# Second part's weights decoded during the attention pairs and kept in DRAM; last output products of the first part in two banks

## The chip, the cores and the metric

One core of a Trainium2 chip runs the whole program. The metric is device time in microseconds (us); the kernel before has a median of 967.74 us over 3 runs. Matmuls run on TensorE (PE), elementwise work on VectorE (DVE), ScalarE (ACT) and GpSimd (POOL); SyncE (SP) issues nearly all DMAs.

## The reference, cut to what matters

```python
# 1. attention: B=4, H=8, S=768, D=48, a recurrence over t
cur = einsum('bhd,bhe->bhde', u * k_t, v_t)
y_t = einsum('bhd,bhde->bhe', r_t, state + cur)
state = w_t[..., None] * state + einsum('bhd,bhe->bhde', k_t, v_t)
# 2. first part, x = y as [3072, 384], d_ff 1536
x = (sigmoid(x @ w_gate) * (x @ w_val)) @ w_out
# 3. second part, d_ff 2048
h = x @ w_in;  g = h * tanh(softplus(h));  out = g @ w_out2
```

The weights arrive as 64-bit floats. The kernel has no 64-bit arithmetic: it rebuilds each weight from the two 32-bit words and stores it as two fp16 numbers (a high part and the rest), with three products where one would do.

## The kernel before, in words

**Stages.** The sequence is cut into 24 steps of 32 tokens, two steps make a pair, and 12 pairs (p = 0 to 11) run one behind another. While the gates of pair p are computed, the attention of pair p + 1 is. For each pair there are 12 gates (`gate(p, f)`, 18 matmuls each, L880, then sigmoid L891 and cast L908 on ACT, product L896 and rest L911 on DVE). The output products of the pair before (`out1(p - 1, c, part)`, L944) run between the gates: three column blocks c of four parts each, accumulated in one PSUM bank, `po`. Each block is split into two fp16 halves (`xo`, L212 on ACT, L215 on DVE) and stored in the DRAM tensor `x2d`; the next block can only start when `xo` has left the bank.

**Attention of a pair.** Products and sums of the short-range part on POOL and DVE (L486, L506), transposes on DVE, scaled copies (L623), scores `lp` on PE (L638), copies of them into `X` on ACT and DVE in turn (L655), rows out `yp` on PE (L728), split `xs` (L212, L215), a transposing DMA on ACT's queue into `xt` (L762), and the state `s`: outer products `kp` on PE (L824), added on DVE (L835), decayed on POOL or DVE (L804).

**Second part.** `open_a` gives the space of the attention's short-range tiles to `wi` (tile `wis`), `open_b`, behind all of the attention, gives the rest to `wp` (tile `wps`), the x tiles and two more PSUM pools. `tail_end()`, called in pair 10, loads and decodes `wi` (8 blocks) and then `wp` (8 blocks, each also combined into the seven operands of a Strassen-like product). `h_unit(r, f)` (L1054) and `out2(r, m, h)` (L1169) then use them.

**Decoding a block** (`load_raw`, `decode`, `combine`): a 768 KB DMA (L267); two ACT passes, `word` (L248) and `low` (L238); a DVE join (L292); for `wi` a cast (L303, ACT or DVE) and a difference (L306, POOL or DVE); for `wp` three sums (L332, `sum_wp`, on POOL or DVE), three casts (L346) and three differences (L332, `wps`).

**Order.** `Plan` is a list scheduler written out in the kernel. Each step is added with an engine (or a choice of engines with costs), a cost, a latency `lat` that follows it, and the keys it reads and writes. `run()` works out how late each step may start, counted back from the end, then gives each engine's next free time to the ready step that is due first, and finally emits all steps by planned begin. On the chip each engine then takes its instructions strictly in that order. `SEM = 0.1` us is the usual latency between steps.

Of the kernel before, what the change touches and what calls it, by code (L numbers as in the profile page):

```python
# [19 lines left out]
NP = NJ // 2  # L20
# [17 lines left out]
SG = 64.0  # L38
SG2 = 64.0
NPT = 32  # L40
NRAW = 1
YPOS = (4, 7)
SEM = 0.1
SHARED = (0,)
WHOLE = range(1, 12, 2)
COLD = 1.9
PARTS = ((), (0,), (1,), (2, 3))
# [2 lines left out]
ENGS = ("pool", "dve")  # L50
W1HI = {"act": 0.83}
W1LO = {"dve": 1.6, "pool": 1.85}
W2HI = {"act": 0.83, "dve": 0.7}
W2LO = {"pool": 1.65, "dve": 0.92}
HD = DM // 2
ORDER = ("11", "12", "S2", "S3", "S1", "22", "S4")
OPERAND = {"11": 0, "12": 1, "S4": 2, "S1": 3, "S3": 4, "S2": 5, "22": 6}
# [102 lines left out]
def mixer_moe_kernel(  # L160
# [30 lines left out]
    pp = sa.enter_context(tc.tile_pool(name="pp", bufs=1, space=PS, side="right"))  # L191

    x2d = dram.tile([NP, KC, 128, 2, NT], F16, name="x2d")
    floor3 = keep.tile([128, 1], F32, name="floor3")
    wgs = w1p.tile([128, 2, KC, F1], F16, name="wgs")
    wvs = w1p.tile([128, 2, KC, F1], F16, name="wvs")
# [62 lines left out]
        npg[0] += 1  # L259
        return ("pg", npg[0] % n)  # L260

    def load_raw(key, pool, src, n, slot, reads=()):
# [6 lines left out]
        add("sp", 2.2, go, reads, [("raw", slot)], lat=2.0)  # L269

    def decode(key, dst, n, count, slot, reads, high_on, lo_on, halves=False, blocks=None):
# [28 lines left out]

        def high(e):
            put = nc.scalar.copy if e == "act" else nc.vector.tensor_copy
            put(out=dst()[:, 0], in_=words[key])  # L303

        def rest(e):
            engines[e].tensor_tensor(  # L306
                out=dst()[:, 1], in0=words.pop(key), in1=dst()[:, 0], op=ALU.subtract
            )

        full = 1.15 if key[0] == "wo" else 0.95  # L310
        add("act", 0.78, rebase, [raw, "consts", "table1"], [word])
        add("act", 1.1, bits3, [raw, "consts"], [low])
        add("dve", full, join, [low], [word])
        if halves:
            combine(key, dst, word, low, reads, high_on, lo_on, count)
            return
        made = [[(key[0], f, a) for f in blocks or [key[1]]] for a in range(2)]
        add(high_on, 0, high, [word, *reads], made[0])
        add(lo_on, 0, rest, [word, *made[0]], made[1])

    def combine(key, dst, word, low, reads, high_on, lo_on, count):
# [12 lines left out]
        def differ(e):  # L334
            sums[key] = t = dp.tile(
                [128, 4, HD], F32, tag=f"low{count % 2}", name=f"sum_{key[0]}{key[1]}"
            )
            w = words[key]
            sub(e, t[:, :2], w[:, :, HD:], w[:, 0].rearrange("p (t d) -> p t d", t=2))
            sub(e, t[:, 2], w[:, 1, HD:], t[:, 0])  # L340
            sub(e, t[:, 3], w[:, 1, :HD], t[:, 2])

        def high(e, n):
            copy = nc.scalar.copy if e == "act" else nc.vector.tensor_copy
            out = dst()[:, 0, 0] if n == 0 else dst()[:, 0, put(n)]
            copy(out=out, in_=blocks(n))  # L346

        def rest(e, n):
            ab = [dst()[:, a, 0] if n == 0 else dst()[:, a, put(n)] for a in range(2)]
            sub(e, ab[1], blocks(n), ab[0])  # L350

        add({"pool": 1.8, "dve": 1.1}, 0, differ, [word], [low])
        for n, part in ((0, 0.25), (1, 0.5), (2, 1.0)):
            src = low if n == 2 else word
            cost = {e: c * part + 0.1 for e, c in high_on.items()}
            add(cost, 0, lambda e, n=n: high(e, n), [src, *reads], [(*key, 0, n)])
            cost = {e: c * part + 0.1 for e, c in lo_on.items()}
            add(cost, 0, lambda e, n=n: rest(e, n), [src, (*key, 0, n)], [(*key, 1, n)])

    def decode_early(name, i, dst, src, count):  # L360

# [504 lines left out]
    def gate(p, f):  # L866
# [63 lines left out]
        add("dve", 0.35, rest, [ps, (*G, 0)], [(*G, 1)])  # L930

    def out1(p, c, part):
        last = p == NP - 1
        bank = "po2" if last and c == 1 else "po"
        cs = slice(128 * c, 128 * c + 128)
        fr = range(3 * part, 3 * part + 3)

# [56 lines left out]
    def open_a(e):  # L994

        sf.close()
        w2["i"] = sb.enter_context(tc.tile_pool(name="w2i", bufs=1))
        w2["wi"] = w2["i"].tile([128, 2, KC, F2], F16, name="wis")

    def open_b(e):  # L1000
        sa.close()
        w2["p"] = sb.enter_context(tc.tile_pool(name="w2p", bufs=1, side="right"))
        w2["raw"] = sb.enter_context(tc.tile_pool(name="raw", bufs=1, side="right"))
        w2["ph"] = sb.enter_context(tc.tile_pool(name="ph", bufs=1, space=PS, side="right"))
        w2["po"] = sb.enter_context(tc.tile_pool(name="po2", bufs=1, space=PS, side="right"))
        w2["wp"] = w2["p"].tile([128, 2, 7, NF2 // 2, HD], F16, name="wps")
        w2["h"] = sb.enter_context(tc.tile_pool(name="hp", bufs=1, side="right"))

    homes = []
    spare = list(range(78))  # L1010
# [30 lines left out]
    def h_unit(r, f):  # L1041
# [1 line left out]
        k = nh[0] % 4  # L1043
        nh[0] += 1
        E = ("e", k)
        fs = slice(128 * f, 128 * f + 128)

        def sums(e):
            t = pg.tile([128, 2, NT], F32, tag=f"pg{ps[1]}", name=f"h{r}_{f}")
# [2 lines left out]
            for a, c in ((0, 0), (0, 1), (1, 0)):  # L1052
                for kc in range(KC):
                    nc.tensor.matmul(  # L1054
                        hps[r, f],
                        w2["wi"][:, a, kc, fs],
                        x2[r][:, c, kc, :],
                        start=(n == 0),
                        stop=(n == 3 * KC - 1),
                    )  # L1060
                    n += 1
# [5 lines left out]
        w = [("wi", f // 2, a) for a in range(2)]  # L1067
        add("pe", 1.95, sums, [*w, ("x2", r % 2)], [ps])
        add("act", 0.62, unit, [ps, "table2", "open"], [E])

# [73 lines left out]
    def out2(r, m, h):  # L1144
# [13 lines left out]
        def sums(e):  # L1158
# [8 lines left out]
            for i in range(NF2 // 2):  # L1167
                for a, c in ((0, 0), (1, 0), (0, 1)):
                    nc.tensor.matmul(  # L1169
                        ops2[h, first],  # L1170
                        home(slots[r, i, name])[:, c, tsl],
                        w2["wp"][:, a, w, i, :],
                        start=(new and n == 0),
                        stop=(n == 3 * NF2 // 2 - 1),
                        skip_group_check=not new,
# [19 lines left out]

        if m == 0 and h == 0:
            add("none", 0, start, [], [O])
        n = {0: 0, 1: 1, 2: 1}.get(w, 2)
        reads = [("slot", slots[r, i, name], c) for i in range(NF2 // 2) for c in range(2)]
        reads += [("wp", i, a, n) for i in range(NF2 // 2) for a in range(2)]  # L1200
# [83 lines left out]
    def tail_end():  # L1284
# [1 line left out]
        done += [("pt", i) for i in range(5)] + [("A", i) for i in range(8)] + ["A"]  # L1286
        add("none", 0, open_a, [], [*done, "opened"])
        for i in range(8):
            cs = slice(256 * i, 256 * i + 256)
            dst = lambda cs=cs: w2["wi"][:, :, :, cs]  # L1290
            load_raw(("wi", i), lambda: dp, in_cols(wi, cs), (KC, 256), i % 3)
            decode(("wi", i), dst, (KC, 256), i, i % 3, ["opened"], W2HI, W2LO)
        add("none", 0, open_b, [], ["attention", "open"])
        for i in range(8):
            cs = slice(2 * i, 2 * i + 2)
            dst = lambda i=i: w2["wp"][:, :, :, i]
            slot = (i + 2) % (3 + NRAW)
            pool = (lambda: dp) if slot < 3 else (lambda: w2["raw"])
            reads = [] if slot < 3 else ["open"]
            load_raw(("wp", i), pool, in_rows(wo2, cs), (2, DM), slot, reads)  # L1300
            decode(("wp", i), dst, (2, DM), i, slot, ["open"], W2HI, W2LO, True)

    cells = {0: fine(0)}
    tail1(0)
# [2 lines left out]
    for p in range(NP):  # L1307
        for f in range(NF1):
# [94 lines left out]
```

## Time and profile before

| | us |
|---|---|
| median of 3 runs | 967.74 |
| lowest, highest | 966.28, 967.86 |
| the profiled execution, its own time | 966.43 |
| its span, first to last instruction | 964.7 |

The page says how long each engine was busy; the list of windows says it stretch by stretch, with the granted clock of TensorE; the list of waits says what PE's idle time ended with. A matmul's duration contains the time it spends in the pipeline, so 18 matmuls of 256 columns issue in about 2 us though each is listed with some 0.27 us.

### The profile page before, as it was taken

How to read it: one execution, taken by the hardware profiler on the slowest of the kernel's cores; microseconds unless marked ns; L12 is line 12 of the kernel's file. 1: busy time of each engine (PE TensorE's matmuls, PEld its weight loads, DVE VectorE, ACT ScalarE, POOL GpSimd, SP SyncE). 2: the span in 40 equal slices, each digit the busy share in tenths (PEclk: the TensorE clock that was granted, in tenths of full speed). 3: DMA queues.
4: the chain of work that ended last, by engine and by line, in shares of the span. 5: the costliest groups of instructions: out<-in, count | busy, mean ns of one | idle time of the engine just before them, and what ended most of it. 6: DMA issues, size and time to landing. Idle time of an engine off the chain costs nothing.

```text
span 964.7 us, 29601 instructions
## 1 busy us (share of the span) xinstructions
PE 895.7 (93%) x12808; PEld 715.9 (74%) x12808; DVE 663.6 (69%) x1202; ACT 496.4 (51%) x1191; POOL 490.7 (51%) x534
## 2 busy tenths in 40 slices
PE   0667899999999999999999889999999999999998
PEld 0455678888888888888888777657767676776788
DVE  7889976767676757686778798875565655556541
ACT  2757864343525344343536566775565655656540
POOL 7999832626464545546364365654343443444330
PEclk9988899999999999999999999999999999999999
DMA  9445832322232323133223760010100102000000
GB/s 307 152 139 163 265 115 75 65 67 72 68 57 72 83 62 76 50 75 71 60 41 101 169 204 12 8 43 1 38 30 10 58 1 66 2 9 26 1 34 34
DMA packets 56467, 71.92 MB, mean 75 GB/s; under 512 B 20752, under 2 KB 37648, under 8 KB 56208
## 3 DMA queue, kind: packets, MB, share of 16 engines
q1 hardware_dynamic: 39696, 66.09, 23.6%
q10 hardware_dynamic: 16640, 3.94, 2.1%
q8 instruction: 100, 1.64, 0.7%
q14 instruction: 31, 0.25, 0.1%
HBM read 56.64 MB, written 9.44 MB: 68 GB/s over the span
## 4 chain that ended last, share of the span: by engine, by line
PE 72%; DVE 13%; ACT 7%; POOL 3%; issue 2%; ACTq 2%; DMA 1%; SPq 0%; DVEq 0%; POOLq 0%
PE gv L880 20%; PE h L1054 19%; PE o L1169 17%; PE o L944 10%; PE yp L728 3%; ACT X L655 2%; ACTq L762 2%; ACT KK L697 2%; DVE X L655 1%; DVE A L506 1%; PE lp L638 1%; POOL pt L486 1%; DVE gt L911 1%; PE kp L824 1%; DVE s L835 1%
## 5 line engine op out<-in xcount | busy, mean ns | idle before, releaser
L1054 PE MATMUL h<-x,wis 128*128 128x512 f16 x864 | 199.9, 379 | 0.0
L486 POOL TENSOR_TENSOR blk<-blk 128x384 f32<-128x384 f32 (+2 forms) x139 | 129.4, 943 | 97.6 <-DMA blk<-rkw 69.9
L880 PE MATMUL gv<-xt,wgs 128*128 128x256 f16 x1296 | 165.9, 278 | 12.3 <-DVE gt L911 11.9
L944 PE MATMUL o<-gt,wos 128*128 128x256 f16 x1296 | 165.2, 273 | 5.9 <-DVE xo L215 5.9
L1088 POOL TENSOR_TENSOR sum<-e 128x256 f32<-128x256 f32 x96 | 71.5, 744 | 186.3 <-ACT e L1065 186.2
L880 PE MATMUL gv<-xt,wvs 128*128 128x256 f16 x1296 | 163.6, 276 | 2.5 <-DVE wvs L306 1.2
L880 PEld LDWEIGHTS <-wgs 128*128 128x128 f16 x1296 | 126.3, 100 | 31.4 <-issue 12.9
L1054 PEld LDWEIGHTS <-wis 128*128 128x128 f16 x864 | 83.5, 98 | 82.9
L944 PEld LDWEIGHTS <-wos 128*128 128x128 f16 x1296 | 126.0, 98 | 24.5 <-issue 6.8
L880 PEld LDWEIGHTS <-wvs 128*128 128x128 f16 x1296 | 125.0, 99 | 20.9 <-DVE wvs L306 1.5
L486 POOL TENSOR_TENSOR pt<-blk 128x384 f32<-128x384 f32 x93 | 105.4, 1157 | 47.0 <-DMA blk<-rkw 43.6
L891 ACT ACTIVATE sig<-gv 128x256 f32<-128x256 f32 x144 | 53.5, 385 | 118.2 <-PE gv L880 114.3
L1065 ACT ACTIVATE e<-h 128x512 f32<-128x512 f32 x96 | 57.2, 596 | 84.6 <-PE h L1054 83.7
L911 DVE TENSOR_TENSOR gt<-gv,gt 128x256 f16<-128x256 f32 x144 | 58.8, 417 | 51.6 <-ACT gt L908 50.1
L908 ACT CAST gt<-gv 128x256 f16<-128x256 f32 x144 | 52.6, 371 | 75.9 <-DVE gv L896 55.3
L896 DVE SCALAR_TENSOR_TENSOR gv<-gv,sig 128x256 f32<-128x256 f32 x144 | 60.7, 431 | 29.3 <-ACT sig L891 28.8
L1169 PE MATMUL o<-wps,gt 128*128 128x192 f16 x612 | 74.0, 246 | 0.0
L655 ACT COPY X<-lp 24x64 f32<-24x64 f32 x174 | 44.5, 256 | 38.2 <-DVE X L655 28.1
L1107 DVE SCALAR_TENSOR_TENSOR gt<-e,gt 128x256 f16<-128x256 f32 x41 | 27.3, 675 | 49.6 <-ACT gt L1102 49.6
L506 DVE TENSOR_REDUCE A<-pt 128x32 f32<-128x768 f32 (+1 forms) x60 | 51.4, 863 | 12.3 <-POOL pt L486 12.3
L1169 PE MATMUL o<-wps,wgs 128*128 128x192 f16 x498 | 59.4, 246 | 0.0
L1169 PE MATMUL o<-wps,wos 128*128 128x192 f16 x456 | 57.1, 246 | 0.0
(106 smaller groups left out, 1508.4 us busy)
## 6 DMA issues: line engine op xcount, KB each, us to landing
v<-vt SPq DMA_DIRECT2D x96, 96.0 KB, 3.3
blk<-rkw SPq DMA_DIRECT2D x22, 384.0 KB, 3.5
raw_wi<-wi SPq DMA_DIRECT2D x8, 768.0 KB, 4.8
raw_wp<-wo SPq DMA_DIRECT2D x8, 768.0 KB, 6.2
blk<-rkw SPq DMA_DIRECT2D x11, 512.0 KB, 4.0
raw_wg<-wg SPq DMA_DIRECT2D x6, 768.0 KB, 6.2
raw_wv<-wv SPq DMA_DIRECT2D x6, 768.0 KB, 6.1
raw_wo<-wo SPq DMA_DIRECT2D x6, 768.0 KB, 4.7
```

The source lines that it names most:

```text
L486: engines[e].tensor_tensor(out=pv, in0=a, in1=b, op=ALU.mult)
L506: nc.vector.tensor_reduce(out=cell(), in_=shape(pts.pop(n)), op=ALU.add, axis=AX.X)
L655: put(out=xp[p][rs, xs, t:], in_=lps[p, e][rs, :, c : c + C - t])
L880: nc.tensor.matmul(gps[p, f][:, o], w[:, a, kc, fs], xt[p][:, c, kc, :], start=(n == 0), stop=(n == 3 * KC - 1),)
L891: nc.scalar.activation(out=sgs[p, f], in_=gps[p, f][:, 0], func=AF.Sigmoid, scale=1.0 / (SW * SX))
L896: nc.vector.scalar_tensor_tensor(out=gps[p, f][:, 1], in0=gps[p, f][:, 1], scalar=SG / (SW * SX), in1=sgs.pop((p, f)), op0=ALU.mult, op1=A ...
L911: nc.vector.tensor_tensor(out=gt[p][:, 1, f], in0=gps[p, f][:, 1], in1=gt[p][:, 0, f], op=ALU.subtract,)
L944: nc.tensor.matmul(ops[p, c][:, :NT], wos[:, a, f, cs], gt[p][:, g, f, :], start=(f == 0 and n == 0), stop=(f == NF1 - 1 and n == 2),)
L1054: nc.tensor.matmul(hps[r, f], w2["wi"][:, a, kc, fs], x2[r][:, c, kc, :], start=(n == 0), stop=(n == 3 * KC - 1),)
L1065: nc.scalar.activation(out=es[r, f], in_=hps[r, f], func=AF.Mish, scale=ih)
L1088: engines[e].tensor_tensor(out=sums[0][:, n - 1], in0=a(), in1=b(), op=op)
L1169: nc.tensor.matmul(ops2[h, first], home(slots[r, i, name])[:, c, tsl], w2["wp"][:, a, w, i, :], start=(new and n == 0), stop=(n == 3 * NF2 ...
```

## The change

The decode steps of `wi` and `wp` move from `tail_end()` into pairs 3 to 9, counted from 0 (the 4th to the 10th). One block is started every five gates, behind the gate's rest (`("tick", p, f)`). It is decoded into a staging tile (tag `raw2`), stored in a DRAM scratch (`wid`, `wpd`) and fetched from there when the space of the second part is open. The decode steps get `lat = SLACK = 3.0` in the plan, so that the steps that follow each other are planned at least 3 us apart. The casts are fixed to ACT, the differences and sums to POOL. The fourth raw slot goes. The tiles `wis` and `wps` get their block number as the first free dimension. Of the output products of pairs 10 and 11 every other block uses bank `po2`.

```diff
-NRAW = 1
+AHEAD = 3
+SLACK = 3.0
-W2HI = {"act": 0.83, "dve": 0.7}
-W2LO = {"pool": 1.65, "dve": 0.92}
+W2HI = {"act": 0.83}
+W2LO = {"pool": 1.65}
+    wid = dram.tile([8, 128, 2, KC, 256], F16, name="wid")
+    wpd = dram.tile([8, 128, 2, 7, HD], F16, name="wpd")
...
-        add("act", 0.78, rebase, [raw, "consts", "table1"], [word])
-        add("act", 1.1, bits3, [raw, "consts"], [low])
-        add("dve", full, join, [low], [word])
+        add("act", 0.78, rebase, [raw, "consts", "table1"], [word], lat)
+        add("act", 1.1, bits3, [raw, "consts"], [low], lat)
+        add("dve", full, join, [low], [word], lat)
...
-        add({"pool": 1.8, "dve": 1.1}, 0, differ, [word], [low])
+        add("pool", 2.4, differ, [word], [low], lat)
...
+    def decode_ahead(name, i, src, n, made, store, tick):
+        key = (name, i)
+        count = 8 * (name == "wp") + i
+        slot = count % 2
+        stage = ("raw", 2)
...
+        add("none", 0, new, [], [stage])
+        load_raw(key, lambda: dp, src, n, slot, [tick], 3 * SLACK)
+        decode(
+            key, lambda: tiles[0], n, count, slot, [stage], W2HI, W2LO, name == "wp", None, SLACK
+        )
...
+        add(
+            "sp",
+            0.6,
+            lambda e: nc.sync.dma_start(out=store[i], in_=tiles[0]),
+            [*parts, stage],
+            [(name, "stored", i)],
+            lat=2.0,
+        )
...
     def out1(p, c, part):
-        last = p == NP - 1
-        bank = "po2" if last and c == 1 else "po"
+        bank = "po2" if p > NP - 3 and (KC * p + c) % 2 else "po"
...
+    def fetch(name, src, i, opened):
+        def go(e):
+            nc.sync.dma_start(out=w2[name][:, i], in_=src[i])
+
+        made = [(name, i)]
+        add("sp", 0.6, go, [(name, "stored", i), opened], made, lat=2.5)
...
         for i in range(8):
-            cs = slice(256 * i, 256 * i + 256)
-            dst = lambda cs=cs: w2["wi"][:, :, :, cs]
-            load_raw(("wi", i), lambda: dp, in_cols(wi, cs), (KC, 256), i % 3)
-            decode(("wi", i), dst, (KC, 256), i, i % 3, ["opened"], W2HI, W2LO)
+            fetch("wi", wid, i, "opened")
         add("none", 0, open_b, [], ["attention", "open"])
         for i in range(8):
...
-            load_raw(("wp", i), pool, in_rows(wo2, cs), (2, DM), slot, reads)
-            decode(("wp", i), dst, (2, DM), i, slot, ["open"], W2HI, W2LO, True)
+            fetch("wp", wpd, i, "open")
...
+            n, rem = divmod(NF1 * (p - AHEAD) + f, 5)
+            if rem == 2 and 0 <= n < 16:
+                ahead(n, ("tick", p, f))
```

## Rows read from the trace of the kernel before

**Rows 1.** The page, part 1: busy time of the engines, share of the span.
```profile
PE 895.7 (93%) x12808; PEld 715.9 (74%) x12808; DVE 663.6 (69%) x1202; ACT 496.4 (51%) x1191; POOL 490.7 (51%) x534
```

**Rows 2.** Windows: length; busy PE, PEld, DVE, ACT, POOL; clock; DMA share; GB/s.
```profile
160.00:344.00 184.00, 183.12 (x3426) 158.73 (x3423) 130.89 (x245) 76.13 (x215) 93.94 (x98) 1.00 0.27 68
344.00:505.00 161.00, 158.57 (x3195) 136.61 (x3195) 113.28 (x218) 65.53 (x188) 86.26 (x90) 1.00 0.27 63
505.00:560.00 55.00, 51.50 (x849) 44.26 (x847) 43.84 (x74) 33.35 (x72) 20.43 (x18) 1.00 0.58 148
560.00:597.00 37.00, 32.74 (x297) 28.80 (x295) 33.43 (x53) 22.18 (x45) 26.02 (x27) 1.00 0.28 92
597.00:964.70 367.70, 364.45 (x2988) 261.18 (x2986) 208.62 (x405) 199.38 (x465) 147.03 (x192) 1.00 0.08 24
```

**Rows 3.** What PE waited for from 344 to 505 us: total, times, longest.
```profile
PE yp L728 <- DVE s L835: 1.3, 4, 0.6
PE yp L728 <- DVE RD L623: 1.0, 2, 0.6
```

**Rows 4.** The same from 505 to 560 us, then from 560 to 597 us.
```profile
PE gv L880 <- issue: 1.6, 2, 1.2
PE yp L728 <- issue: 1.4, 2, 0.7
PE yp L728 <- DVE s L835: 0.5, 2, 0.3
...
PE o L944 <- DVE xo L215: 4.3, 3, 2.3
```

**Rows 5.** Groups by shape from 160 to 505 us: one per gate.
```profile
L911 DVE TENSOR_TENSOR gt<-gv,gt 128x256 f16<-128x256 f32 x94 | 38.1, 417 | 42.5 <-ACT gt L908 41.0
```

**Rows 6.** Timeline of ACT and PE in pair 2 (153 to 158 us).
```profile
154.94 1.01 ACT L238 ACTIVATE low_wi<-raw_wi,floor 128x768 uint32<-128x768 uint16 x1
...
157.94 0.27 PE L944 MATMUL o<-gt,wos 128*128 128x256 f16 x1 [0.95 <-DVE xo L215]
```

**Rows 7.** Groups by shape, whole span: decode steps, count, busy, mean ns, idle before.
```profile
L306 POOL TENSOR_TENSOR wis<-word_wi,wis 128x768 f16<-128x768 f32 x6 | 10.1, 1684 | 19.8 <-DVE wis L303 14.7 <-ACT wis L303 5.1
L332 POOL TENSOR_TENSOR sum_wp<-word_wp,sum_wp 128x192 f32<-128x192 f32 x16 | 11.9, 745 | 1.3
L332 POOL TENSOR_TENSOR sum_wp<-word_wp 128x384 f32<-128x384 f32 x8 | 8.9, 1116 | 13.1 <-DVE word_wp L292 13.1
L332 POOL TENSOR_TENSOR wps<-sum_wp,wps 128x768 f16<-128x768 f32 x3 | 5.5, 1818 | 0.9 <-ACT wps L346 0.9
L238 ACT ACTIVATE low_wi<-raw_wi,floor 128x768 uint32<-128x768 uint16 x8 | 8.1, 1011 | 4.8 <-issue 4.7
```

**Rows 8.** Tile word_wi: count, duration ns min/median/max, first and last start.
```profile
L292 DVE SCALAR_TENSOR_TENSOR word_wi<-word_wi,low_wi x8: 947/1127/2404, 150.2 to 540.9; 128x768 uint32<-128x768 uint32 x8
L303 ACT CAST wis<-word_wi x2: 832/836/840, 520.6 to 543.3; 128x768 f16<-128x768 f32 x2
```

**Rows 9.** Groups by shape from 505 to 560 us: a decode step, the gate's cast.
```profile
L248 ACT ACTIVATE word_wi<-raw_wi 128x768 f32<-128x768 f32 x6 | 5.5, 916 | 0.0
L908 ACT CAST gt<-gv 128x256 f16<-128x256 f32 x13 | 4.6, 374 | 5.3 <-DVE word_wi L292 3.0 <-DVE gv L896 2.2
```

**Rows 10.** Timeline of one attention, without decode steps (347 to 351 us).
```profile
347.86 1.67 ACT L655 COPY X<-lp 24x64 f32<-24x64 f32 x6 [0.24 <-PE lp L638]
349.80 0.15 PEld L728 LDWEIGHTS yp<-v,X 64*32 64x32 f32 x8 [0.21 <-ACT X L655]
```

**Rows 11.** Tile xt: landing min/median/max from 160 to 560 us, then from 505 us.
```profile
DMA to landing us min/median/max: 2.3/4.0/8.9
...
DMA to landing us min/median/max: 5.1/7.0/8.9
```

**Rows 12.** Timeline of ACT and PE in pair 7: the last sends, the next pair's first gate.
```profile
409.62 2.59 ACTq L762 DMA_TRANSPOSE xt<-xs  x2
...
421.05 2.13 PE L880 MATMUL gv<-xt,wgs 128*128 128x256 f16 x18
```

More of the change, by code (lines that the diff above doesn't have):

```diff
@@ L260, in next_pg, with load_raw @@
         return ("pg", npg[0] % n)
-    def load_raw(key, pool, src, n, slot, reads=()):
+    def load_raw(key, pool, src, n, slot, reads=(), lat=2.0):
         def go(e):
@@ L267, in go, with decode @@
             nc.sync.dma_start(out=raws[key], in_=src)
-        add("sp", 2.2, go, reads, [("raw", slot)], lat=2.0)
-    def decode(key, dst, n, count, slot, reads, high_on, lo_on, halves=False, blocks=None):
+        add("sp", 2.2, go, reads, [("raw", slot)], lat=lat)
+    def decode(key, dst, n, count, slot, reads, high_on, lo_on, halves=False, blocks=None, lat=SEM):
         raw = ("raw", slot)
@@ L310, in decode, with combine @@
         full = 1.15 if key[0] == "wo" else 0.95
-        add("act", 0.78, rebase, [raw, "consts", "table1"], [word])
-        add("act", 1.1, bits3, [raw, "consts"], [low])
-        add("dve", full, join, [low], [word])
+        add("act", 0.78, rebase, [raw, "consts", "table1"], [word], lat)
+        add("act", 1.1, bits3, [raw, "consts"], [low], lat)
+        add("dve", full, join, [low], [word], lat)
         if halves:
-            combine(key, dst, word, low, reads, high_on, lo_on, count)
+            combine(key, dst, word, low, reads, high_on, lo_on, count, lat)
             return
         made = [[(key[0], f, a) for f in blocks or [key[1]]] for a in range(2)]
-        add(high_on, 0, high, [word, *reads], made[0])
-        add(lo_on, 0, rest, [word, *made[0]], made[1])
-    def combine(key, dst, word, low, reads, high_on, lo_on, count):
+        add(high_on, 0, high, [word, *reads], made[0], lat)
+        add(lo_on, 0, rest, [word, *made[0], *reads], made[1], lat)
+    def combine(key, dst, word, low, reads, high_on, lo_on, count, lat):
         sums = {}
@@ L355, in combine, with new @@
             cost = {e: c * part + 0.1 for e, c in high_on.items()}
-            add(cost, 0, lambda e, n=n: high(e, n), [src, *reads], [(*key, 0, n)])
+            add(cost, 0, lambda e, n=n: high(e, n), [src, *reads], [(*key, 0, n)], lat)
             cost = {e: c * part + 0.1 for e, c in lo_on.items()}
-            add(cost, 0, lambda e, n=n: rest(e, n), [src, (*key, 0, n)], [(*key, 1, n)])
+            add(cost, 0, lambda e, n=n: rest(e, n), [src, (*key, 0, n), *reads], [(*key, 1, n)], lat)
+    def decode_ahead(name, i, src, n, made, store, tick):
[3 more added lines that the diff above has]
+        stage = ("raw", 2)
+        tiles = []
+        def new(e):
+            t = dp.tile([128, 3072], F16, tag="raw2", name=f"made_{name}{i}")
+            size = 2
+            for k in made:
+                size *= k
+            names = "abcd"[: len(made) + 1]
+            dims = {x: k for x, k in zip(names, (2, *made))}
+            tiles.append(
+                t[:, :size].rearrange(f"p ({' '.join(names)}) -> p {' '.join(names)}", **dims)
+            )
[4 more added lines that the diff above has]
+        )
+        if name == "wp":
+            parts = [(*key, a, k) for a in range(2) for k in range(3)]
+        else:
+            parts = [(*key, a) for a in range(2)]
+        add(
[5 more added lines that the diff above has]
+            lat=2.0,
+        )
     def decode_early(name, i, dst, src, count):
@@ L929, in gate @@
             add("act", 0.34, high, [ps], [(*G, 0), *room])
-        add("dve", 0.35, rest, [ps, (*G, 0)], [(*G, 1)])
+        add("dve", 0.35, rest, [ps, (*G, 0)], [(*G, 1), ("tick", p, f)])
     def out1(p, c, part):
-        last = p == NP - 1
-        bank = "po2" if last and c == 1 else "po"
+        bank = "po2" if p > NP - 3 and (KC * p + c) % 2 else "po"
         cs = slice(128 * c, 128 * c + 128)
@@ L997, in open_a @@
         w2["i"] = sb.enter_context(tc.tile_pool(name="w2i", bufs=1))
-        w2["wi"] = w2["i"].tile([128, 2, KC, F2], F16, name="wis")
+        w2["wi"] = w2["i"].tile([128, 8, 2, KC, 256], F16, name="wis")
     def open_b(e):
@@ L1002, in open_b @@
         w2["p"] = sb.enter_context(tc.tile_pool(name="w2p", bufs=1, side="right"))
-        w2["raw"] = sb.enter_context(tc.tile_pool(name="raw", bufs=1, side="right"))
         w2["ph"] = sb.enter_context(tc.tile_pool(name="ph", bufs=1, space=PS, side="right"))
         w2["po"] = sb.enter_context(tc.tile_pool(name="po2", bufs=1, space=PS, side="right"))
-        w2["wp"] = w2["p"].tile([128, 2, 7, NF2 // 2, HD], F16, name="wps")
+        w2["wp"] = w2["p"].tile([128, 8, 2, 7, HD], F16, name="wps")
         w2["h"] = sb.enter_context(tc.tile_pool(name="hp", bufs=1, side="right"))
+    def fetch(name, src, i, opened):
[3 more added lines that the diff above has]
+        add("sp", 0.6, go, [(name, "stored", i), opened], made, lat=2.5)
     homes = []
@@ L1045, in h_unit @@
         E = ("e", k)
-        fs = slice(128 * f, 128 * f + 128)
+        fs = slice(128 * (f % 2), 128 * (f % 2) + 128)
         def sums(e):
@@ L1055, in sums @@
                         hps[r, f],
-                        w2["wi"][:, a, kc, fs],
+                        w2["wi"][:, f // 2, a, kc, fs],
                         x2[r][:, c, kc, :],
@@ L1065, in unit @@
             nc.scalar.activation(out=es[r, f], in_=hps[r, f], func=AF.Mish, scale=ih)
-        w = [("wi", f // 2, a) for a in range(2)]
+        w = [("wi", f // 2)]
         add("pe", 1.95, sums, [*w, ("x2", r % 2)], [ps])
@@ L1171, in sums @@
                         home(slots[r, i, name])[:, c, tsl],
-                        w2["wp"][:, a, w, i, :],
+                        w2["wp"][:, i, a, w, :],
                         start=(new and n == 0),
@@ L1197, in out2 @@
             add("none", 0, start, [], [O])
-        n = {0: 0, 1: 1, 2: 1}.get(w, 2)
         reads = [("slot", slots[r, i, name], c) for i in range(NF2 // 2) for c in range(2)]
-        reads += [("wp", i, a, n) for i in range(NF2 // 2) for a in range(2)]
+        reads += [("wp", i) for i in range(NF2 // 2)]
         add("pe", 1.95, sums, reads, [bank])
@@ L1288, in tail_end, with ahead @@
         for i in range(8):
-            cs = slice(256 * i, 256 * i + 256)
-            dst = lambda cs=cs: w2["wi"][:, :, :, cs]
-            load_raw(("wi", i), lambda: dp, in_cols(wi, cs), (KC, 256), i % 3)
-            decode(("wi", i), dst, (KC, 256), i, i % 3, ["opened"], W2HI, W2LO)
+            fetch("wi", wid, i, "opened")
         add("none", 0, open_b, [], ["attention", "open"])
         for i in range(8):
-            cs = slice(2 * i, 2 * i + 2)
[L1296 to L1299, printed above, removed]
-            load_raw(("wp", i), pool, in_rows(wo2, cs), (2, DM), slot, reads)
-            decode(("wp", i), dst, (2, DM), i, slot, ["open"], W2HI, W2LO, True)
+            fetch("wp", wpd, i, "open")
+    def ahead(n, tick):
+        i = n % 8
+        if n < 8:
+            cs = slice(256 * i, 256 * i + 256)
+            decode_ahead("wi", i, in_cols(wi, cs), (KC, 256), (KC, 256), wid, tick)
+        else:
+            cs = slice(2 * i, 2 * i + 2)
+            decode_ahead("wp", i, in_rows(wo2, cs), (2, DM), (7, HD), wpd, tick)
     cells = {0: fine(0)}
```

## The prediction

> **What bounds the kernel now.** The page's busy times come first: PE is busy for 93% of the span, DVE for 69%, ACT and POOL for about half [rows 1]. Such an average hides stages, so the windows come next, and what is to be seen there is PE's busy time against the length of each stretch [rows 2]. From 160 to 344 us PE loses 0.9 of 184 us, in the next 161 us 2.4, and behind 597 us 3.3, which is the drain at the end. Between them lie 92 us in which it loses 3.5 and 4.3. The granted clock is 1.00 in all five stretches, 2.4 GHz, so none of this is owed to the clock. The list of waits names the losses. From 344 to 505 us they are 2.3 us in six waits of the attention's `yp` [rows 3]. From 505 to 560 us they are 3.5 us, around the attention again, and from 560 to 597 us three waits of the output products for `xo`, 4.3 us, the longest 2.3 [rows 4]. In that last stretch DVE is busy for 33.4 of 37 us, 90%, against 57% afterwards [rows 2]: the second part's weights are decoded there. So the change has some 8 us to win, 0.8%. PE's own work stays the same, instruction for instruction.
>
> **What it removes.** The decode steps leave the stretches from 505 to 597 us, whose waits are 3.5 + 4.3 = 7.8 us [rows 4]. The 4.3 us have two cures in the change: DVE gets free, and the next block of products no longer needs the bank that `xo` still reads. I take all of it as gone. Of the 3.5 us, pair 11's attention keeps what a pair loses without decode steps: a pair is 12 gates of 345/94 = 3.67 us, 44 us [rows 5], and 2.3 us in 161, or in 3.7 pairs, is 0.6 us a pair [rows 3]. Some `wi` steps also ran in pair 2. There an ACT pass of 1.0 us starts at 154.9 us, sigmoid, cast and `xo` come behind it, and PE waits 0.95 us for that `xo` [rows 6]. Nothing is decoded in pair 2 afterwards, so this 0.9 us goes as well.
>
> **What it adds, by engine.** A `wi` block costs ACT `low` 1.01, `word` 0.92 and a cast of 0.84, 2.8 us; DVE one join of 0.95 to 2.40, median 1.13; POOL one difference of 1.68 [rows 7 to 9]. A `wp` block costs ACT the same two passes and three casts of 1344 columns together, 1.5 us at the rate of that cast of 768 and 1.7 with something for two instructions more: 3.6 us. POOL gets all of its sums, 1.12 + 2 × 0.75 = 2.6 us, and its differences, 0.75 + 1.12 + 1.82 = 3.7 us by the rows of those shapes: 6.3 us [rows 7]. One block starts every five gates, 18.4 us. In pairs 6 to 9, where `wp` falls, this makes ACT 41% + 20% = 61%, DVE 70% + 6% = 76%, POOL 54% + 34% = 88% while it lasts, 85% over the 161 us (86.3 + 8 × 6.3 = 137) [rows 2]. None reaches PE's 98%. By throughput the steps lie beside PE's work and cost nothing; nothing waits for them until the fetches, so the plan gives them gaps.
>
> **What it costs by order.** Each engine takes its steps in the planned order, and a decode step of 1 to 2 us that stands ahead of a late one of the attention delays it. The cover is thin: the last copies of `X` end at 349.5 us, `yp`, which reads them, starts at 349.8, and PE's weight load has waited for them already [rows 10]. Behind a decode step on ACT or DVE stand the copies into `X`, the addition to `s`, sigmoid, casts and `xo`; for these wait `yp`, the gates' banks and the next block of products. What this costs per block no row shows alone. The lower end is 0: from 160 to 344 us PE lost 0.9 us with DVE at 71%, so a full engine does not by itself stop it [rows 2]. The upper end is pair 2's 0.95 us behind one block's passes, 16 × 0.95 = 15.2 us [rows 6]. Nearest is the stretch from 505 to 560 us, the same steps beside the same attention, six blocks of `wi`: (3.5 - 0.6)/6 = 0.48 us a block, 7.7 us for 16 [rows 4, 9]. But there ACT also stood still for 3.0 us, because its next cast was queued behind a decode step that waited for a join [rows 9]; steps planned 3 us apart should not do this, and one block in 18 us is less crowded than six in 55. I take half, 0.25 us a block, 4.0 us.
>
> **Queues.** SP gets 16 loads of 768 KB, 16 stores and 16 fetches. A load waits for its gate and a raw slot, a store for the block's last difference, and behind them stand the loads of `blk` and `v` and the stores of `x2d`. The store is planned 3 us behind that difference, so SP stands still only where POOL is later than this. I cost it at nothing; without that cover POOL starts a pair's short-range products later, and the price is bounded by 0 and the 2.4 us of one POOL step a pair, seven times, 17 us, of which I take 0 since the row nearest, the quiet pairs, shows no wait of PE for them [rows 3]. The sends of `xt` share the DMA engines with the loads. They land after 2.3 to 8.9 us, 4.0 in the median, and 5.1 to 8.9 beside the raw loads from 505 us on [rows 11]. In pair 7 both of the last sends are issued by 412.2 us, the second about 411.0, and PE turns to a gate of the next pair at 421.05 at the earliest [rows 12]; even the longest landing, at 419.9, is in time. The fetches move 8.7 MB (16 tiles of 393 or 688 KB). At the 148 GB/s of the crowded stretch that is 58 us [rows 2]; `wis` is already open to writes at 520.6 us [rows 8], so they end by 579 us, ahead of the second part at 597. The new layout of `wis` and `wps` keeps whole the rows that PE reads; I cost it at nothing.
>
> **The sum.** 966.4 (the profiled execution) - 7.8 + 0.6 - 0.9 + 4.0 = 962.3 us. The median of the three runs, 967.7, is 1.3 us above that execution, so 963.6 us.
>
> **POOL beside DVE.** The join of `wi` took 0.95 to 2.40 us with POOL at work beside it [rows 8], and POOL's 768-column difference took 1.82 us for `wps` against 1.68 for `wis`, 8% more, in the stretch with the busier DVE [rows 7]. The Trainium skill (GPSIMD Engine Reference, Key points) says that GpSimd shares its SBUF interfaces with VectorE and contends with DVE instructions in a 2-port mode or with two SBUF inputs; that speaks against moving 6.3 us of POOL work beside a DVE at 70%, and by that rule alone the sum would be the second rival's 973.3 us. The rows agree that the durations spread, but not that they spread by as much as that takes.
>
> **The rivals.** With L for the loss per block the time is 959.6 + 16 L.
>
> *Displacement at pair 2's price.* Steps on ACT delay the copies into `X` and `xo` as in pair 2: L = 0.95, 959.6 + 15.2 = 974.8 us, slower. It decides from L = 0.63, where 16 L passes the 8.1 us won by the 1.9 us that count. The wait in pair 2 speaks for it, the 0.48 of the dense stretch against it. Chance 0.1.
>
> *POOL becomes the bound in pairs 6 to 9.* At 85% its steps must take 1/0.85 = 1.18 times as long before the attention's scaled copies are late for good. The rows show 1.08. At 1.25, a little above the 1.19 of DVE's join between its shortest and its median [rows 8], POOL is at 106%, 0.06 × 161 = 9.7 us on top, 973.3 us. Chance 0.08.
>
> *The dense stretch's price holds*, L from 0.39 to 0.63, 965.8 to 969.7 us, with 967.3 at 0.48. Chance 0.18.
>
> *The wait only changes its name*: the last pairs stay as slow because a fetch, or `open` itself, comes late; 967.7 us. The 18 us between the fetches' end and 597 us speak against it. Chance 0.05.
>
> *The gain comes whole*, L near 0, perhaps with some of the 2.4 us of pairs 6 to 9: 957.5 to 960.4 us. Chance 0.16.
>
> **How the numbers follow.** The forecast, L from 0.05 to 0.39, holds the rest, 0.43; its own range is 960.4 to 965.8 us. A measurement of this kernel tells a change of 0.2%, 1.9 us, from none. Below 965.8 us lie the forecast and the whole gain, 0.59; within 0.2% the dense price and the changed name, 0.23; above 969.7 us the two slower rivals, 0.18. The range for 8 in 10 goes from 957.5 us, the whole gain, to 970.5, just past the dense price; it leaves out most of the slower rivals.
>
> **What would show it.** Right: no wait of `o` for `xo` behind 545 us, DVE well under 90% in the last pair, the first `h` some 5 us earlier, and in pairs 3 to 9 a few new waits of `yp`, `kp` or `o`, each below 1 us, 4 us in all. Wrong: new waits of over 8 us in those pairs, waits of `lp` for `RD` (POOL late), ACT idle behind decode steps, SP standing at a store, or a wait of `gv` for `xt`.

## The result, and the profile after

The changed kernel takes 974.85 us (median of six runs, 971.12 to 977.07) against 966.15 us of the kernel before on the same chip (six runs, 965.13 to 967.86). The ratio is 1.0082, 95% interval 1.0066 to 1.0099: slower by 0.8%, where 963.6 us, faster, was forecast. The profiled execution took 971.75 us, its span 970.0.

The first view is the page's busy times, the second the windows of [rows 2], with 970.0 as the end.

```profile
PE 896.1 (92%) x12808; PEld 717.0 (74%) x12808; DVE 647.6 (67%) x1178; ACT 500.5 (52%) x1195; POOL 514.3 (53%) x554
...
HBM read 65.29 MB, written 18.09 MB: 86 GB/s over the span
```

```profile
160.00:344.00 184.00, 179.10 (x3390) 155.08 (x3388) 135.65 (x245) 84.70 (x219) 103.82 (x104) 1.00 0.39 107
344.00:505.00 161.00, 153.44 (x3040) 132.00 (x3037) 121.47 (x223) 86.60 (x219) 116.89 (x116) 1.00 0.45 131
505.00:560.00 55.00, 52.41 (x975) 44.95 (x967) 34.76 (x66) 25.09 (x67) 31.07 (x35) 1.00 0.39 133
560.00:597.00 37.00, 37.00 (x342) 33.17 (x340) 12.04 (x30) 10.12 (x29) 0.00 (x0) 1.00 0.56 204
597.00:970.00 373.00, 369.76 (x3036) 265.88 (x3033) 208.12 (x404) 199.93 (x465) 147.06 (x192) 1.00 0.07 24
```

Length minus PE's busy time tells the story. In the stretch before the second part PE now loses nothing where it lost 4.3 us, and DVE is busy for 12.04 us where it was for 33.4 [rows 2]; from 505 to 560 us PE loses 2.6 instead of 3.5. But from 160 to 344 us it loses 4.9 instead of 0.9, and up to 505 us 7.6 instead of 2.4. That is 9.2 us lost anew in the pairs and 5.2 won at their end, 4.0 net; PE has also done 0.9 us less work by 160 us, and its busy time grew by 0.4. Together these are the 5.3 us between the spans, 970.0 and 964.7. They are complete when the second part begins: its first `h` starts at 602.0 us instead of 596.7.

The list of PE's waits, from 160 to 505 us and then from 505 to 600, names them.

```profile
PE yp L768 <- DVE RD L663: 4.6, 4, 2.2
PE yp L768 <- DVE s L875: 3.5, 5, 2.7
PE gv L920 <- DVE gt L951: 2.3, 1, 2.3
PE yp L768 <- issue: 1.0, 1, 1.0
PE gv L920 <- issue: 0.9, 1, 0.9
PE yp L768 <- DVE X L695: 0.3, 1, 0.3
...
PE gv L920 <- issue: 1.3, 1, 1.3
PE yp L768 <- DVE s L875: 1.1, 2, 0.9
PE yp L768 <- issue: 0.2, 1, 0.2
```

The kernel before, from 160 to 505 us ([rows 3] begin at 344):

```profile
PE yp L728 <- DVE RD L623: 1.8, 3, 0.7
PE yp L728 <- DVE s L835: 1.3, 4, 0.6
```

The waits of `o` for `xo` [rows 4] are gone. In the pairs stand 12.6 us of waits where 3.1 stood, and they are few and long: 13 waits, five of the attention's `yp` for `s` and four for `RD`, the longest 2.7 us. That longest one, in the timeline of ACT, DVE and PE:

```profile
268.75 1.00 ACT L241 ACTIVATE low_wi<-raw_wi,floor 128x768 uint32<-128x768 uint16 x1
...
269.66 0.91 ACT L251 ACTIVATE word_wi<-raw_wi 128x768 f32<-128x768 f32 x1
...
270.46 0.48 ACT L215 ACTIVATE xs<-yp 128x384 f16<-128x384 f32 x1
...
270.97 3.54 ACTq L802 DMA_TRANSPOSE xt<-xs  x2
...
274.56 0.37 ACT L948 CAST gt<-gv 128x256 f16<-128x256 f32 x1 [3.34 <-issue]
274.96 0.42 DVE L951 TENSOR_TENSOR gt<-gv,gt 128x256 f16<-128x256 f32 x1 [3.09 <-ACT gt L948]
275.30 1.01 DVE L875 TENSOR_TENSOR s<-kp,s 128x384 f32<-128x384 f32 x2
...
275.91 0.27 PE L768 MATMUL yp<-s,RD 64*32 64x48 f32 x2 [2.72 <-DVE s L875]
```

The last `yp` of that attention ended at 267.7 us, but two passes of a decode step (1.9 us) stood ahead of `xs` on ACT. Two sends of `xt` follow `xs`; they hold ACT's queue until 274.5 us, in which it computes nothing ("3.34 <-issue"). Only then comes the gate's cast; DVE's product waits for it, the addition to `s` is queued behind that product, and PE waits 2.72 us for `s`. So a step's 1.9 us on ACT, together with sends that took 3.5 us, reaches PE through ACT's cast and two steps of DVE.

The profiled execution is 3.1 us under the median. A second profile of the same kernel, taken in the rerun below, shows what some of its executions add; the columns are those of the windows above, the granted clock behind the busy times.

```profile
270.00:276.00 6.00, 3.52 (x109) 2.80 (x100) 2.90 (x7) 1.00 (x3) 4.48 (x6) 1.00 0.42 104
276.00:280.00 4.00, 4.00 (x64) 2.83 (x56) 3.06 (x5) 1.14 (x3) 3.92 (x4) 0.60 0.02 4
...
446.00:452.00 6.00, 3.53 (x102) 2.66 (x94) 3.18 (x11) 4.23 (x14) 5.84 (x7) 0.91 0.19 75
452.00:456.00 4.00, 4.00 (x94) 3.19 (x86) 1.69 (x5) 1.46 (x3) 0.83 (x1) 0.71 0.02 6
```

Behind these two stretches, in which PE was busy for only 3.5 of 6 us, its granted clock falls to 0.60 and 0.71, that is, from 2.4 to 1.2 GHz for part of the next 4 us. Then PE is "busy" and does 0.60 × 4 us of work: 1.6 and 1.2 us that no list of waits shows. PE's busy time is 2.8 us longer than in the first profile, for the same instructions. In that first profile the same place lost as much, and the clock stayed:

```profile
270.00:276.00 6.00, 3.28 (x91) 2.70 (x82) 1.93 (x5) 1.59 (x4) 4.31 (x5) 1.00 0.46 108
276.00:280.00 4.00, 3.81 (x139) 3.15 (x140) 3.59 (x5) 0.77 (x3) 3.60 (x3) 1.00 0.02 4
```

So such a stall lowers the clock in some executions and not in others. Of the six runs the two with a mean granted clock of 0.988 and 0.989 took 971.75 and 971.12 us, the four at 0.980 to 0.984 took 974.83 to 977.07. That the clock makes the 3.1 us is likely from this, not shown: with the sends' price of 2.5 (below) the two runs of the lowest clock, 0.977 and 0.975, are the two fastest.

### The profile page after: what moved, and what is told of

It reads as the page before. It is cut to its first block, busy times and chain, and to the rows that moved or that the text cites. A ratio compares the mean times of both kernels' runs of the same rounds, so it can differ in the third digit from the quotient of the medians.

```text
span 970.0 us, 29672 instructions
## 1 busy us (share of the span) xinstructions
PE 896.1 (92%) x12808; PEld 717.0 (74%) x12808; DVE 647.6 (67%) x1178; ACT 500.5 (52%) x1195; POOL 514.3 (53%) x554
## 4 chain that ended last, share of the span: by engine, by line
PE 63%; DVE 13%; POOL 10%; ACT 6%; DMA 4%; issue 3%; ACTq 1%; SPq 0%; POOLq 0%; DVEq 0%
PE h L1099 19%; PE o L1214 17%; PE gv L920 15%; PE o L983 8%; POOL blk L526 4%; POOL pt L526 4%; ACT KK L737 2%; DVE X L695 2%; ACT X L695 2%; PE yp L768 2%; DVE gt L951 1%; DVE KT L728 1%; DMA blk<-rkw 1%; DMA raw_wv<-wv 1%; DVE KD L644 1%
## 5 line engine op out<-in xcount | busy, mean ns | idle before, releaser
L526 POOL TENSOR_TENSOR pt<-blk 128x384 f32<-128x384 f32 x93 | 110.3, 1211 | 42.8 <-DMA blk<-rkw 37.6
L695 ACT COPY X<-lp 24x64 f32<-24x64 f32 x159 | 40.7, 256 | 36.6 <-DVE X L695 30.5
L737 ACT COPY KK<-KT 32x384 f32<-32x384 f32 x96 | 48.9, 509 | 14.6 <-DVE KT L728 13.3
```

The source lines that it names most:

```text
L526: engines[e].tensor_tensor(out=pv, in0=a, in1=b, op=ALU.mult)
L695: put(out=xp[p][rs, xs, t:], in_=lps[p, e][rs, :, c : c + C - t])
L737: nc.scalar.copy(out=whole, in_=own)
```

## The experiments

The theory: decode steps on ACT, queued ahead of the attention, make the new waits. Its rivals: the DMA traffic alone; POOL's steps beside DVE; the place of the steps; the choice of engines; a price of 0.15 us in the plan for sends that hold ACT far longer. Ratios are to the kernel before, run on the same chip.

**The banks alone**, in the kernel before:

```diff
-         last = p == NP - 1
-         bank = "po2" if last and c == 1 else "po"
+         bank = "po2" if p > NP - 3 and (KC * p + c) % 2 else "po"
```

> The kernel before with the two banks alone; the weights are decoded in the last pairs as before. It shows which cure removed the 4.3 us of waits for xo behind 560 us. If the bank was the cause: those waits are gone though DVE stays at 90%, and the time is 962 us. If DVE was the cause: the products get their bank but the gates behind them wait for DVE instead, the waits move to gv, and the time is within 1 us of 966. Any theory: nothing changes ahead of 545 us.

Measured: 966.21 us, ratio 1.0003 (0.9988 to 1.0018). Its waits of PE from 540 to 600 us:

```profile
PE o L943 <- DVE xo L215: 2.2, 1, 2.2
PE h L1053 <- DVE gt L911: 1.3, 1, 1.3
PE gv L880 <- DVE gt L911: 1.1, 1, 1.1
```

4.3 us of `xo` became 4.6 us of waits for DVE, as was expected if DVE is the cause. The bank alone is no cure; with another change it becomes one, at the end of this section.

**Halving the change.** First its traffic without its steps (zeros are stored), then its steps without its traffic (only the first two loads of raw weights and one store of each weight):

```diff
...
-        decode(
-            key, lambda: tiles[0], n, count, slot, [stage], W2HI, W2LO, name == "wp", None, SLACK
-        )
...
```

> The changed kernel without the decode steps of wi and wp on ACT, DVE and POOL: the 16 loads, 16 stores and 16 fetches stay, what is stored is zeros, so the second part is computed from zeros. Theory A (decode steps stand ahead of late attention steps in the engines' order): the 9 us that PE lost more from 160 to 505 us go, 2 to 3 us of waits are left there, the time is 960 to 964 us. Theory B (the traffic stretches the sends of xt on ACT's queue and delays blk): the waits stay, 970 to 974 us. Theory C (the plan's new order, not the steps): the 2 us lost ahead of 160 us stay under both.

```diff
-        load_raw(key, lambda: dp, src, n, slot, [tick], 3 * SLACK)
+        if count < 2:
+            load_raw(key, lambda: dp, src, n, slot, [tick], 3 * SLACK)
...
+        if i == 0:
             add("sp", 0.6, lambda e: nc.sync.dma_start(out=store[i], in_=tiles[0]), ...)
```

> The changed kernel with all decode steps, but of the 16 loads only the first two and of the stores only one for each weight; later blocks are decoded from the first two raw tiles, so the second part's weights are wrong copies. The counterpart of the run without steps. Theory A: as slow as the changed kernel, 970 to 975 us. Theory B: 961 to 965 us, no send of xt issues in over 1.3 us, and the 2.7 us wait behind such a send is gone. If both matter: about 968 us.

Then everything but one engine's steps: without POOL's sums and differences (low halves stay zero), and without ACT's passes and casts (two memsets on POOL give the words instead):

```diff
-        add("pool", 2.4, differ, [word], [low], lat)
...
-            add(cost, 0, lambda e, n=n: rest(e, n), [src, (*key, 0, n), *reads], [(*key, 1, n)], lat)
+            add("none", 0, lambda e: None, [src, (*key, 0, n), *reads], [(*key, 1, n)], lat)
```

> The changed kernel without POOL's part of the decoding: the sums and differences are left out, the low halves stored are zeros, the last casts read the word instead of the sums, so the second part's weights are wrong. ACT's and DVE's steps and the traffic stay. If POOL (85% busy in the wp pairs, and contending with DVE) is what costs, 963 to 967 us. If ACT's steps are, 970 us or more.

```diff
-        add("act", 0.78, rebase, [raw, "consts", "table1"], [word], lat)
-        add("act", 1.1, bits3, [raw, "consts"], [low], lat)
...
+            add("pool", 0.8, fixed_word, [raw], [word], lat)
+            add("pool", 0.8, fixed_low, [raw], [low], lat)
...
```

> The changed kernel without ACT's part of the decoding: the two passes are replaced by two POOL memsets a block and the casts are left out, so the second part's weights are zeros. DVE's joins, POOL's sums and differences and the traffic stay. If ACT's 51 us are what costs: the pairs from gate 2 to gate 10 take about 357 us as without any step, and the time is 961 to 965 us. If DVE's joins or the new order cost: 968 us or more.

Measured: traffic alone 961.87 us, 0.9956 (0.9941 to 0.9972); steps alone 967.72, 1.0014 (0.9998 to 1.003); without POOL's steps 971.66, 1.0049 (1.003 to 1.0069); without ACT's 965.44, 0.9991 (0.9975 to 1.0008). The changed kernel once more, in another set of runs:

> The changed kernel itself once more, so that it stands beside the others on one chip. If its 974.9 us are its own, 972 to 977 us here; the run without traffic (967.7) then shows that traffic costs 5 to 9 us beside the decode steps. If 974.9 came from that chip, about 970 us.

Measured: 972.55 us, 1.0069 (1.005 to 1.0088). The window from 160 to 505 us, with the columns of [rows 2], one fence for each kernel: before, after, traffic alone, steps alone, without ACT's steps.

```profile
160.00:505.00 345.00, 341.69 (x6620) 295.34 (x6618) 244.17 (x462) 141.66 (x403) 180.20 (x188) 1.00 0.27 66
```

```profile
160.00:505.00 345.00, 332.55 (x6427) 287.08 (x6424) 257.12 (x468) 171.30 (x437) 220.71 (x220) 1.00 0.42 118
```

```profile
160.00:505.00 345.00, 338.20 (x6583) 292.07 (x6582) 243.40 (x455) 140.45 (x400) 179.09 (x188) 1.00 0.45 126
```

```profile
160.00:505.00 345.00, 336.21 (x6506) 290.01 (x6505) 257.84 (x465) 173.58 (x441) 230.32 (x229) 1.00 0.29 72
```

```profile
160.00:505.00 345.00, 338.21 (x6528) 291.93 (x6525) 265.67 (x476) 135.50 (x388) 255.61 (x263) 1.00 0.44 121
```

PE loses 3.3 us before and 12.5 after; with the traffic alone 6.8, with the steps alone 8.8. So the traffic costs 3.5 us there and the steps 5.5, and the two make up the 9.2. This holds for one execution of each; the second profile of the changed kernel loses 11.2 us where the first loses 12.5. By the medians the halves would add up if the change with neither steps nor traffic took some 957 us (0.9956 + 1.0014 - 1.0069 = 0.9901 of the time before); that kernel was not run. Without ACT's steps 6.8 remain, as with the traffic alone, although DVE's joins still run and POOL is busier than in any other kernel, 255.6 us: what the steps cost in the pairs they cost through ACT. The median, 965.44, is still 3.6 us above that of the traffic alone. The profiles put this ahead of all decode steps of the second part: pair 3's first sigmoid, the 37th, starts at 206.9 us against 202.7.

**The plan.** Less space between a block's steps; fewer and quieter places (two blocks a pair, passes only behind gates 7 and 9); engines free to choose as before the change:

```diff
-SLACK = 3.0
+SLACK = 0.1
...
-        load_raw(key, lambda: dp, src, n, slot, [tick], 3 * SLACK)
+        load_raw(key, lambda: dp, src, n, slot, [tick], 2.0)
```

> The changed kernel with the decode steps planned 0.1 us apart instead of 3 us. If the spacing protects the attention, as the prediction said, ACT stands still behind decode steps that wait for one another and the time rises by 2 to 6 us, to 977 to 981. If what costs is the steps' own length ahead of late ones, spacing or not, the time stays within 2 us of the changed kernel's 974.9.

```diff
...
-            n, rem = divmod(NF1 * (p - AHEAD) + f, 5)
-            if rem == 2 and 0 <= n < 16:
-                ahead(n, ("tick", p, f))
+            if 2 <= p < 10 and f in (7, 9):
+                ahead(2 * (p - 2) + (f == 9), ("tick", p - 1, f + 2), ("tick", p, f))
```

> The changed kernel with the same steps and the same traffic at another place in the pair: two blocks a pair in pairs 2 to 9, their loads behind gates 9 and 11 of the pair before, their first passes only behind gates 7 and 9, when the attention's rows are out, so that most steps lie between one attention and the next. If the steps cost because they stand ahead of the attention's tight part, half or more of the 9 us of waits from 160 to 505 us go, 964 to 968 us. If the amount of work on ACT, DVE and POOL is what costs, wherever it stands, the time stays at 971 to 977 us.

```diff
-W2HI = {"act": 0.83}
-W2LO = {"pool": 1.65}
+W2HI = {"act": 0.83, "dve": 0.7}
+W2LO = {"pool": 1.65, "dve": 0.92}
...
-        add("pool", 2.4, differ, [word], [low], lat)
+        add({"pool": 1.8, "dve": 1.1}, 0, differ, [word], [low], lat)
```

> The changed kernel with casts, differences and sums free to go to ACT or DVE, and to POOL or DVE, as in the kernel before. If POOL at 85% is the bound in the wp pairs, or ACT's casts are what delays the copies into X, the plan takes some to DVE and the time falls by 2 us or more, to 973 or less. If DVE is the tight one, its steps delay s and xo and the time rises by 1 to 4 us.

Measured: 988.37 us, 1.0232 (1.0209 to 1.0256); 971.61, 1.0066 (1.0045 to 1.0086); 975.2, 1.0096 (1.0076 to 1.0116). Neither another place nor other engines help. With the passes behind gates 7 and 9 `yp` still waits 4.4 us for `s`, so no run shows a place in the pair where ACT's steps are free. The spacing is worth 14 to 16 us, more than the 2 to 6 that were expected. ACT's list of waits without it, from 160 to 524 us:

```profile
ACT made_wi L306 <- DVE word_wi L295: 6.6, 3, 3.7
ACT made_wp L349 <- issue: 5.7, 2, 3.8
```

**Half of the work.** Only `wi` ahead, `wp` decoded where the kernel before decodes it:

```diff
...
-            fetch("wp", wpd, i, "open")
...
+            load_raw(("wp", i), pool, in_rows(wo2, cs), (2, DM), slot, reads)
+            decode(("wp", i), dst, (2, DM), i, slot, ["open"], W3HI, W3LO, True)
...
-            if rem == 2 and 0 <= n < 16:
+            if rem == 2 and 0 <= n < 8:
```

> The changed kernel with only wi decoded ahead (8 blocks of 2.8 us ACT, 1.1 us DVE, 1.7 us POOL) and wp in the last pairs as before. By the loss per block of the changed kernel's profile (9.2 us for 16 blocks) the pairs lose 3 to 5 us; the last pairs keep the waits behind 560 us. 966 to 971 us. If wp's 6.3 us of POOL a block were the cost, the pairs lose under 2 us and the time is 963 to 966.

Measured: 964.62 us, 0.9981 (0.9966 to 0.9996), below the 966 to 971 that were expected. With half of the blocks the gain at the end outweighs the loss in the pairs, by 0.2%.

**The price of a send.** In the timeline above two sends hold ACT for 3.5 us, and the plan counts 0.15 for both. With 2.5 in its place, in the changed kernel, in the kernel before, and in the kernel with `wi` alone ahead:

```diff
-            attn("act", 0.15, send, [*reads, *room], new, lat=2.8)
+            attn("act", 2.5, send, [*reads, *room], new, lat=2.8)
```

> The changed kernel, with the two sends of xt planned at 2.5 us of ACT's time instead of 0.15. In the traces they hold ACT for 1.2 us each, up to 2.4 beside a load, and the longest waits of yp for s follow such a pair of sends: the gate's cast stands behind them, DVE's addition to s behind the cast. If the plan's wrong cost turns the decode steps into waits, the 3.5 us of yp for s and part of the rest go and the time falls by 3 to 8 us, to 965 to 970. If it is the steps' own length, it stays at 971 to 975.

> The kernel before with the same planned cost of the sends. It has 1.3 us of such waits in the pairs and 0.5 us in the last. If the cost matters only together with the decode steps: within 1 us of before. If it matters by itself: 964 or less.

> Only wi ahead, and the sends planned at 2.5 us. The run with wi only had 3.1 us of waits of yp for s in the pairs and 964.6 us. If the planned cost is the cause of these: 961 to 963 us. If not: 964 to 966.

Measured: 974.03 us, 1.0067 (1.0049 to 1.0086); 961.01, 0.9938 (0.9914 to 0.9961); 965.0, 0.9986 (0.9972 to 0.9999). The plan's price is no cure for the change: `yp` no longer waits for `s`, but `kp` waits 3.6 us for `X` and `o` 2.6 for `xo`, and PE loses 13.3 us from 160 to 505. The kernel before gains 0.6%. More than half of what its profile gains, 3.6 of 6.9 us, lies ahead of pair 3 (the 37th sigmoid at 201.2 us, before 204.8), where no list here says why. With the price, the copies of `X` on ACT alone, in the changed kernel and in the one before, so that ACT and DVE no longer wait for each other in turn:

```diff
-                attn({"act": 0.82, "dve": 0.93}, 0, lambda on, e=e, n=n: merge(on, e, n), [banks[e]], [X[e][n]])
+                attn({"act": 0.82}, 0, lambda on, e=e, n=n: merge(on, e, n), [banks[e]], [X[e][n]])
```

> The changed kernel with the sends planned at 2.5 us and all eight groups of copies into X on ACT, where the plan before gives them to ACT and DVE in turn. If the loss comes through these copies, because a decode step ahead of either engine's turn holds both, the waits of yp, kp and gv behind them go and the time falls to 962 to 968 us. If ACT is simply too full (6.5 us a pair more on it, some 65% busy), it rises above 974.

> The kernel before with the sends planned at 2.5 us and the copies into X on ACT alone. With that cost the kernel before has 1.1 us of waits left in the pairs. If copies in turn cost nothing where no decode step stands beside them: 960 to 962 us. If they cost by themselves: 959 or less; if ACT is too full: above 962.

Measured: 974.39 us, 1.0076 (1.0051 to 1.0102), and 963.48, 0.9968 (0.9952 to 0.9984). In the changed kernel the wait of `kp` for `X`, 3.6 us, becomes three for `KK`, 3.1 us, also ACT's work. And the price with the two banks, in the kernel before:

> The kernel before with the sends planned at 2.5 us and the two banks. The sends' cost alone gave 961.0 us, with 4.0 us of one wait of o for xo left. If the bank holds that wait: 957 to 959. If DVE does, as the run with two banks alone said: 960 to 962.

Measured: 956.96 us (six runs, 953.9 to 959.5), 0.9907 (0.9883 to 0.9932). It is the fastest of all kernels here, and no decode step is moved in it. Its waits of PE from 160 to 505 us, then to 600:

```profile
PE yp L728 <- DVE RD L623: 2.6, 4, 0.7
...
PE gv L880 <- issue: 2.3, 1, 2.3
PE h L1053 <- DVE gt L911: 0.6, 1, 0.6
PE yp L728 <- issue: 0.2, 1, 0.2
```

No `yp` waits for `s` any more [rows 3], and no `o` for `xo` [rows 4]: the first is the price's doing, since the kernel with the price alone has none of the former either, but 4.0 us of the latter. That the banks, worth nothing alone, help once the price is right is likely: the wait for `xo` goes, as was expected if the bank holds it, though DVE is busy for 29.7 of 37 us from 560 us on. The intervals of the two, 0.9938 and 0.9907, overlap.

## Why the prediction was wrong

The profiled executions, 966.43 and 971.75 us, differ by +5.3 us where 4.1 us less was forecast, and these are the terms, forecast and measured: the waits at the end, -7.2 and -5.2; pair 2, -0.9 and +0.9 by 160 us; order and queues together, +4.0 and +9.2; PE's busy time, 0 and +0.4. The distance from the profiled execution to the median, 1.3 and 3.1, gives the remaining 1.8 of the 11.2 us by which the forecast was off.

- **What it removes** held up to its size. The waits for `xo` are gone and DVE is at 33% in the last pair; 5.2 us were won where 7.2 were forecast, since 2.6 us of waits stay around pair 11's attention, 1.5 of them for PE's own instructions, where 0.6 was expected. That the gain has "two cures" was half right: the bank alone gave nothing, and took the wait away only beside the right price of the sends. The 0.9 us of pair 2 are not to be seen; at 160 us PE is 0.9 us of work further back, with 14.6 us of `gv <- gt` from 60 to 160 us where there were 11.9. But the kernel with the banks alone, whose edit touches only the last pairs, started pair 2's first sigmoid (the 25th) at 158.5 us where the one before started it at 160.2 and the changed one at 162.2: differences of this size come in the front without an edit in it. They seem to go with the kernel and its plan, since both profiles of the changed kernel have pair 3's first sigmoid late, at 206.7 and 206.2 us against 204.8. Why stays open.
- **What it adds, by engine** held: no engine became the bound. POOL was at 73% from 344 to 505 us, not 85%, since a block's steps spread over more time, and without ACT's steps it took 74% of the longer window at no loss beyond that of the traffic.
- **"Queues. I cost it at nothing."** This step failed, and it is the larger part of the 5.2 us by which the pairs were off: the traffic alone costs 3.5 us there. 2.6 of it are waits for PE's instructions, which the prediction did not think of; about 1 us is more of the waits for `s` and `RD`. Landing times held, and there is no PE wait for `xt` or `wis`. SP stood for 21.2 us at stores, and no listed PE wait is for what stood behind them. That the traffic stretches the sends of `xt` is not shown: they took up to 2.42 us in the changed kernel, but also 2.18 with the steps alone and 2.09 before.
- **"What it costs by order": "I take half, 0.25 us a block".** The mechanism held and the size was too low. The steps alone cost 5.5 us, 0.34 a block, where 4.0 were forecast; with the traffic it is 9.2 us, 0.57 a block. The dense stretch's 0.48, loads and steps together, was the nearest row and nearly right; I halved it because a block in 18 us is less crowded than six in 55 and steps 3 us apart "should not do this". The spacing does what it is for: without it 988.37 us. But two passes are enough where ACT is just then on the attention's chain, as in the timeline from 268.75 us on. The listed waits for `s`, `RD`, `gt` and `X` grew by 7.6 us, 0.48 a block.
- **POOL beside DVE** fell. Taking all of POOL's steps away left 971.66 us, 1.0049, and the interval of that just holds the rerun's 1.0069: 0.2%, some 2 us, which the noise covers. The joins of `wi` took 0.93 to 1.75 us, median 1.28, with POOL's steps and 0.92 to 1.75, median 1.21, without them. The Trainium skill (GPSIMD Engine Reference, Key points) has GpSimd contend with DVE instructions that have two SBUF inputs. The joins here agree with it only by 0.07 us in the median, and not in the longest. The 973.3 us of that rival is close to the median for another reason.
- **A missing term** is probably the clock: it was read as 1.00 from before, and no step asked what a wait of 2 to 3 us does to it. The median lies 3.1 us above the profiled execution, and the second profile shows granted clocks of 0.60 and 0.71 right behind such waits. That it makes the whole difference is not shown.

The rival whose number came nearest, displacement at pair 2's price with 974.8 us, came there by luck: it wants 0.95 us a block, and 0.57 were measured, below the 0.63 from which it decides. By the loss per block it was the dense stretch's price that held, whose 965.8 to 969.7 us miss because the end, the front and the median's distance went wrong as well. Its kind of cost, steps on ACT that delay the attention, is what the runs show.

## What to carry to other kernels

A step moved beside a saturated engine is not free because the other engines have room: ask, for each engine that takes it, whose next link stands behind it, and price it by a row where such a step stood ahead of such a link, traffic included. Halve a change, traffic against steps and engine by engine; here PE's lost time of the halves added up to the whole within 0.2 us, in one execution of each. And compare a plan's prices with the trace before moving work about: putting one wrong price right (0.15 for what holds ACT 2.4 us) gained 0.6% where the change lost 0.8%.

## What the runs showed of the hardware

PE's waits for "issue" fall where a block of its instructions arrives late. Queue 8 moves them (packets, MB, share, in the page's list of queues of the changed kernel):

```profile
q8 instruction: 100, 1.64, 0.7%
```

These are 100 packets of 16 KB. PE and PEld have 2 × 12808 = 25,616 instructions, and with the semaphore instructions in PE's stream the trace has 25,713: 100 × 256 and 113. Counted in that stream, every such wait of over 0.1 us behind 160 us, in all profiles here, stands 193 or 194 instructions behind a multiple of 256, and it ends 1.2 to 2.4 us after such a packet landed. An example, in the changed kernel's timeline of PE, amid eight equal products:

```profile
314.50 0.26 PE L768 MATMUL yp<-v,X 64*32 64x48 f32 x7
315.71 0.20 PE L768 MATMUL yp<-v,X 64*32 64x48 f32 x1 [0.96 <-issue]
```

From 160 to 505 us they occur in eleven of the twelve profiles with the second part's traffic (not in the one without ACT's steps), and not in the kernel whose steps run without it, nor in the kernel before, which has them from 505 us on, beside its own loads [rows 4]. That the weights' packets delay the instruction packets is argued from this; no run separates it further.
